# Attention output divided with features on partitions instead of after a transpose, and a half-precision product with wo

## The chip, the cores and the metric

The kernel runs on one core of a Trainium2 chip. Its engines are TensorE (PE in the profile, its weight loads PEld), VectorE (DVE), ScalarE (ACT), GpSimd (POOL) and SyncE (SP), which here issues DMAs. The metric is the device time of one execution in microseconds.

## The reference

Two blocks run one after the other on a sequence of 2048 tokens with 448 features: attention with 16 heads of 28 features, and a product-key mixture of experts that reads its result. Shapes: `x` 1 x 2048 x 448, `wqkv` 448 x 1344, `wo` 448 x 448.

```python
def _A_ref(x, wqkv, wo):
    B, S, D = x.shape
    H = 16
    Dh = D // H
    qkv = (x @ wqkv).reshape(B, S, 3, H, Dh).transpose(2, 0, 3, 1, 4)
    q, k, v = qkv[0], qkv[1], qkv[2]
    scores = jnp.einsum("bhqd,bhkd->bhqk", q, k) * (Dh ** -0.5)
    p = _softmax(scores, axis=-1)
    o = jnp.einsum("bhqk,bhkd->bhqd", p, v)
    return o.transpose(0, 2, 1, 3).reshape(B, S, D) @ wo
...
h = x + _A_ref(_layernorm(x), A_wqkv, A_wo)
h2 = h + _B_ref(_layernorm(h), B_w_q, B_k1, B_k2, B_u, B_v)   # 16 heads, two key tables of 64, top 8, 4096 experts
```

## The kernel before

**Stages.** First queries, keys and values are projected and written to memory (to about 155 us of the span). Then the attention runs (155 to 829 us), with much other work woven into it. After it come the rest of the mixture's preparation and the expert products.

**The attention.** The generator `attention` makes 256 steps: 16 blocks n, each with 16 key tiles k. Block n is a pair b, g: 512 queries (b, four of them) and four heads (g, four groups). Step u issues the scores of step u + 2 (L565, 12 matmuls on row tiles), the two exponentials for them (L569, on ScalarE) and the values of step u (L592, column tiles, accumulated in one PSUM bank called A over the 16 steps of a block). The four heads of a block lie on partitions 32j to 32j + 31: 28 features, then on row 32j + 28 the sum of the exponentials (values carry a column of ones), then three zeros. At some steps, the `paired` ones, the values of the following step run too. The scores have room for one and a half steps in PSUM.

**Dividing (`finish`, L572).** After a block's last step VectorE copies A to SBUF (`o`, L597). Two steps into the next block TensorE transposes `o` in four pieces into the PSUM bank M (L580), VectorE takes the reciprocals of the 16 sums a token now has (L582) and multiplies (L583) into `ob[b]`, tokens on partitions, 448 features. Bank M exists once during the attention and serves all side work: a new user waits until the one before it has been read. `behind_values` says at which steps `finish` is issued behind the values instead of ahead of them.

**The product with wo (`project(b)`, L640).** When the four blocks of b are divided, four tiles of 128 tokens follow, six steps apart. Each loads x, transposes its tile of `ob` (through `transposed` and `turn`, L122, into M), makes a high and a low fp32r part (L659, L136, L137), and multiplies: eleven matmuls of 448 columns with the high and low parts of wo (L93, as `M<-woh,oh`, `M<-wol,oh`, `M<-woh,ol`; the low part has three feature tiles). Then x is added (L680), the row moments taken (L730), a reciprocal root made on GpSimd (L113), and the normed row transposed by DMA (L699). `load_wo` (L627) reads wo in four slices through a tile with two buffers, and VectorE and GpSimd split it. For b = 3 the same runs after the attention, with `room`: more buffers, ScalarE for the copies.

**What is woven.** `weave` runs generators by positions: each has a number of steps and a stretch, and the one with the lowest position goes next. The order that comes out is the order on all engines and on SyncE's queue (manual schedule). Positions in the attention are its steps. Until step 68 (`FOLDED`) the fold of the query weights runs beside it; then from `begin[b]` the projection of b, and 26 steps later the search over the keys (`search`, 16 products of 11 matmuls, one every two steps, with weights loaded at L784 into three buffers, two of which serve one pair of products). `begin` is 73, 133 and 195. Splitting of the expert tables (`part`, on GpSimd), maxima over them (`tops`) and the choice of pairs (`pairs_of`) run beside all this.

**Scales.** `Scale.see` takes a maximum over the columns of a piece (L150), `spread` the maximum over pieces and copies it to a 128 x 128 tile, `share` has TensorE transpose that tile into M (L158) and then takes the overall maximum and makes a power of two from it. The fold's weights and the expert tables use it; wo doesn't.

**The tail.** After step 255: the copy, `finish` of block 15, then `project(3, 2, room)` woven with two first expert products (`first_up`), the first expert weights (`weights(0)`: VectorE compares L973, L979, L994, TensorE L1021) and the last search's scores (`kept_scores`).

## Time and profile before

| | us |
|---|---|
| three runs: median (lowest, highest) | 1591.58 (1589.65, 1596.7) |
| the profiled execution | 1590.46 |
| its span, first to last instruction | 1588.7 |

| engine | busy us in the span | share |
|---|---|---|
| PE | 1532.8 | 96% |
| PEld | 669.4 | 42% |
| DVE | 1146.5 | 72% |
| ACT | 910.0 | 57% |
| POOL | 362.1 | 23% |

The chain that ended last is 74% TensorE and 18% VectorE. These shares are means over stages with different limits, so they don't say what a change in one stage is worth; for that the stretches and the timelines are read. A matmul's row begins when it is issued and its end is modelled, so rows of consecutive matmuls overlap, and the time that one costs is read from the start of one to the start of the next.

### The profile page before, as it was taken

The numbers are of one execution on the slowest core, as the hardware profiler recorded it, in microseconds if no ns is written. First come the engines' busy times: TensorE is split into PE (matmuls) and PEld (weight loads), VectorE is DVE, ScalarE is ACT, GpSimd is POOL, SyncE is SP. The second block draws the span as 40 slices with busy tenths as digits, with TensorE's granted clock in tenths as the row PEclk, the third lists the DMA queues.
The fourth block names the chain that finished last, engine by engine and source line by source line (L and its number), as shares of the span: only waits on it lengthen the run. The fifth ranks groups of instructions, "written<-read, shape, count | busy, mean of one in ns | idle before, by whom it ended". The sixth has DMA issues, their size and how long they took to land.

```text
span 1588.7 us, 33185 instructions
## 1 busy us (share of the span) xinstructions
PE 1532.8 (96%) x12540; PEld 669.4 (42%) x12540; DVE 1146.5 (72%) x3924; ACT 910.0 (57%) x1220; POOL 362.1 (23%) x488
## 2 busy tenths in 40 slices
PE   5999999999999999999998999999999999999999
PEld 3444222233333333333335654455445554555444
DVE  7763365444477867666599899789998999789623
ACT  3544888888888888888873433344423344334322
POOL 1242000534235743787662000000000000000000
PEclk9999999999999999999999999999999999999999
DMA  8424687556677756569733244453344534443444
GB/s 278 141 97 127 224 268 244 173 179 215 213 252 218 245 173 219 165 202 278 225 114 101 91 133 130 130 182 119 105 136 129 158 107 132 141 137 117 121 144 134
DMA packets 170018, 266.10 MB, mean 167 GB/s; under 512 B 25472, under 2 KB 102016, under 8 KB 169856
## 3 DMA queue, kind: packets, MB, share of 16 engines
q1 hardware_dynamic: 165632, 261.88, 52.9%
q10 hardware_dynamic: 4224, 2.10, 0.4%
q8 instruction: 98, 1.61, 0.4%
q14 instruction: 64, 0.52, 0.1%
HBM read 211.88 MB, written 49.28 MB: 164 GB/s over the span
## 4 chain that ended last, share of the span: by engine, by line
PE 74%; DVE 18%; DMA 2%; POOL 2%; issue 2%; ACT 1%; SPq 0%; DVEq 0%; POOLq 0%
PE M L93 14%; PE acc L1234 14%; PE A L592 13%; PE S L565 11%; PE A L93 9%; PE pq L93 6%; DVE p L994 4%; DVE fg L979 2%; DVE G L1015 2%; PE M L273 2%; PE A L1021 1%; DVE ring L1206 1%; DVE f L973 1%; DVE w L1209 1%; PE A L1011 1%
## 5 line engine op out<-in xcount | busy, mean ns | idle before, releaser
L569 ACT ACTIVATE P<-S,escale 128x1024 f32<-128x1024 f32 x512 | 535.7, 1118 | 82.1 <-PE S L565 75.9
L1234 PE MATMUL acc<-v,w 128*128 128x448 f16 x1536 | 308.3, 354 | 1.3 <-DVE w L1209 1.0
L592 PE MATMUL A<-P,V 128*32 128x512 f32 x2048 | 257.6, 601 | 1.3 <-DVE o L597 1.3
L565 PE MATMUL S<-qS,kS 32*128 32x512 f16 x3072 | 230.4, 378 | 2.9 <-ACT P L569 2.2
L1234 PEld LDWEIGHTS <-w 128*128 128x128 f16 x1536 | 148.4, 98 | 143.4 <-DVE w L1209 4.0
L93 PEld LDWEIGHTS <-u 128*128 128x128 f16 x1386 | 131.1, 98 | 146.4 <-issue 6.8
L93 PE MATMUL A<-Xb,u 128*128 128x512 f16 x759 | 178.6, 384 | 2.5 <-DVE G L1015 2.5
L1160 ACT ACTIVATE ring<-A,ugelu 128x512 f32<-128x512 f32 x71 | 48.7, 687 | 218.8 <-PE A L93 218.8
L994 DVE TENSOR_TENSOR p<-st,iota 128x2048 f16<-128x2048 f16 x128 | 156.7, 1225 | 14.9 <-PE M L1011 8.1
L93 PE MATMUL M<-w,Xb 128*128 128x512 f16 x704 | 163.1, 379 | 3.5 <-DVE oh L137 1.6
L1206 DVE SCALAR_TENSOR_TENSOR ring<-ring,wscale,G 128x512 f32<-128x512 f32 x128 | 92.1, 746 | 77.7 <-ACT ring L1160 77.6
L565 PEld LDWEIGHTS <-kS 32*128 32x128 f16 x3072 | 63.6, 92 | 198.3 <-issue 162.7
L93 PE MATMUL M<-Xb,u 128*128 128x512 f16 x627 | 146.4, 379 | 0.0
L93 PEld LDWEIGHTS <-Xb 128*128 128x128 f16 x704 | 64.0, 98 | 92.8 <-issue 20.5
L1208 ACT ACTIVATE w<-ring 128x512 f16<-128x512 f32 x128 | 75.8, 622 | 41.1 <-DVE ring L1206 28.9
L592 PEld LDWEIGHTS A<-P,V 128*32 128x32 f32 x2048 | 48.2, 108 | 120.5 <-issue 110.9
L816 DVE MAX8 ti<-fresh 128x8 f32<-128x64 f32 x384 | 57.3, 212 | 53.8 <-ACT fresh L797 53.6
L1051 POOL TENSOR_SCALAR raw<-raw,scale 128x512 f32<-128x512 f32 (+1 forms) x64 | 47.4, 741 | 188.7 <-PE M L158 145.8
L1209 DVE SCALAR_TENSOR_TENSOR w<-w,ring 128x512 f16<-128x512 f16 x128 | 84.9, 686 | 7.2 <-ACT w L1208 6.9
L1160 ACT ACTIVATE ring<-M,ugelu 128x512 f32<-128x512 f32 x57 | 39.2, 688 | 87.8 <-PE M L93 86.1
L979 DVE TENSOR_TENSOR fg<-f,st 128x2048 f16<-128x2048 f16 x64 | 78.8, 1231 | 0.1
L818 DVE FIND_INDEX8 ti<-ti,fresh 128x8 uint32<-128x64 f32 x384 | 76.9, 220 | 0.0
(197 smaller groups left out, 1897.3 us busy)
## 6 DMA issues: line engine op xcount, KB each, us to landing
v<-vs SPq DMA_DIRECT2D x128, 336.0 KB, 2.9
u<-us SPq DMA_DIRECT2D x126, 256.0 KB, 2.6
w<-wp SPq DMA_DIRECT2D x56, 512.0 KB, 4.9
kS<-ks SPq DMA_DIRECT2D x64, 256.0 KB, 4.9
V<-vd SPq DMA_DIRECT2D x64, 256.0 KB, 3.6
wr<-in_wq_dram SPq DMA_DIRECT2D x32, 448.0 KB, 4.2
vs<-hl SPq DMA_DIRECT2D x32, 336.0 KB, 5.2
seen<-in_uT_dram SPq DMA_DIRECT2D x32, 256.0 KB, 5.0
```

Source lines behind the costliest of these rows:

```text
L93: nc.tensor.matmul(ps, l, r, start=i == 0, stop=i == len(pairs) - 1)
L565: nc.tensor.matmul(S[j // 2][:, j % 2], kS[r, a, 128 * (k % 4):128 * (k % 4) + 128], qS[r, c], start=m == 0, stop=m == 2)
L569: nc.scalar.activation(Pt[:, 2 * i:2 * i + 2], S[i], AF.Exp, scale=escale[:, n % 4:n % 4 + 1])
L592: nc.tensor.matmul(O[n][32 * j:32 * j + 32], V[:, k % 4, j], Pt[:, j], start=k == 0, stop=k == NT - 1)
L818: nc.vector.max_index(i, t, src)
L979: nc.vector.tensor_tensor(fg.rearrange("p t k f u -> p t k (f u)"), f1.rearrange("p t f u -> p t (f u)").unsqueeze(2).to_broadcast([128, T ...
L994: newest[0] = nc.vector.tensor_tensor(p1, pairs(0, s, TG, 128), ids(TG, 128), op=OP.is_equal).ins
L1160: gelu[0] = nc.scalar.activation(act, p, AF.Gelu_apprx_tanh, scale=ugelu).ins
L1206: nc.vector.scalar_tensor_tensor(av, av, wscale, of_expert(b, f), op0=OP.mult, op1=OP.mult)
L1208: nc.scalar.activation(w[:, 0], a, AF.Copy, scale=1.0 / LS)
L1209: newest[0] = nc.vector.scalar_tensor_tensor(w[:, 1], w[:, 0], -LS, a, op0=OP.mult, op1=OP.add).ins
L1234: nc.tensor.matmul(acc[j][:, :D], l, r, start=f == 0 and k == 0, stop=f == 31 and k == 2)
```

## The change

Division moves to where the features still lie on partitions, for 15 of the 16 blocks, and no transpose is made:

- The copy of A goes straight to `on[b]`, 128 x 4 x 512, for all four groups of b.
- `divide(n, k)` runs at the steps k of the following block. At k = 1 the four rows of sums are written to memory (`gather`, four rows of 2 KB).
- For n with n mod 4 = 3, at k = 2 each row of sums is loaded from memory onto its 32 partitions (`spread`, four DMAs), and at k = 4 to 7 VectorE takes the reciprocal of 128 columns and multiplies them (`scale`, four times).
- For the other blocks the 2048 sums are loaded as 128 x 16 at k = 3, inverted at k = 5, written back at k = 6, spread at k = 8, and multiplied at k = 10 over 512 columns.
- The last block has `divide_last`: four matmuls of 4 columns pick the sums out transposed, VectorE inverts and copies them 32 times wide, four transposes bring that back, and VectorE multiplies.
- A product tile takes its 128 columns of `on[b]` as they are: a half-precision copy, a subtraction for the low half, and twelve matmuls of half precision (four feature tiles for each of three products). wo is padded to 4 x 128 rows to match.
- Half precision needs a scale: `load_wo` now loads wo in one DMA, takes four maxima, shares them (with the transpose on TensorE), and splits on VectorE alone, in 9 calls over positions 0 to 8. The inverse scale is applied where x is added.
- `begin` becomes 76, 133 and 197; `behind_values` is gone.

```diff
-        def finish(n, o):
+        def gather(n):
             b, g = divmod(n, 4)
-            if g == 0:
-                ob[b] = (w2 if b % 2 else pp).tile([128, 4, D], F32, name="ob", bufs=1)
+            nc.sync.dma_start(sum_d[n], on[b].rearrange("(j r) g q -> j r g q", r=32)[:, 28, g])
+        def spread(n, src):
+            rb[n] = pp.tile([128, 512], F32, name="rb", bufs=1)
+            for j in range(4):
+                nc.sync.dma_start(rb[n][32 * j:32 * j + 32], src[j:j + 1].to_broadcast([32, 512]))
+        def invert(n, k):
+            flat = (lambda t: t.rearrange("j (k q) -> (j k) q", q=16))
+            if k == 0:
+                rb[n] = pp.tile([128, 16], F32, name="r", bufs=1)
+                nc.sync.dma_start(rb[n], flat(sum_d[n]))
+            elif k == 1:
+                nc.vector.reciprocal(rb[n], rb[n])
+            else:
+                nc.sync.dma_start(flat(rec_d[n]), rb[n])
+        def scale(n, c, inverse):
+            b, g = divmod(n, 4)
+            r, o = rb[n][:, c], on[b][:, g, c]
+            if inverse:
+                nc.vector.reciprocal(r, r)
+            nc.vector.scalar_tensor_tensor(o, o, onscale, r, op0=OP.mult, op1=OP.mult)
+        def divide(n, k):
+            if k == 1:
+                gather(n)
+            if n % 4 == 3:
+                if k == 2:
+                    spread(n, sum_d[n])
+                if 4 <= k < 8:
+                    scale(n, slice(128 * (k - 4), 128 * (k - 3)), True)
+            elif k in (3, 5, 6):
+                invert(n, (3, 5, 6).index(k))
+            elif k == 8:
+                spread(n, rec_d[n])
+            elif k == 10:
+                scale(n, slice(0, 512), False)
+        def divide_last(n):
+            b, g = divmod(n, 4)
+            o = on[b][:, g]
             flush()
-            pt = P[0].tile([128, 4, 4, 32], F32, name="M")
+            pt = P[0].tile([128, 4, 4], F32, name="M")
             for c in range(4):
-                nc.tensor.transpose(pt[:, c].rearrange("p h d -> p (h d)"), o[:, 128 * c:128 * c + 128], ident)
...
+                nc.tensor.matmul(pt[:, c], o[:, 128 * c:128 * c + 128], ct[:, C_SEL:C_SEL + 4], start=True, stop=True)
+            r = pp.tile([128, 4, 4], F32, name="r", bufs=1)
+            nc.vector.reciprocal(r, pt)
+            rr = pp.tile([128, 4, 4, 32], F32, name="rb", bufs=1)
+            nc.vector.tensor_copy(rr, r.unsqueeze(3).to_broadcast([128, 4, 4, 32]))
+            pt = P[0].tile([128, 4, 128], F32, name="M")
+            for c in range(4):
+                nc.tensor.transpose(pt[:, c], rr[:, c].rearrange("p j d -> p (j d)"), ident)
+            nc.vector.scalar_tensor_tensor(o, pt.rearrange("p c q -> p (c q)"), onscale, o, op0=OP.mult, op1=OP.mult)
...
     def load_wo():
...
+        S = Scale("o", 4)
+        raw = w2.tile([128, 4, 512], F32, name="on", bufs=1)...
+        nc.sync.dma_start(raw, wo)
+        yield
+        yield
+        for g in range(4):
+            S.see(g, raw[:, g])
+        yield
+        yield from S.share()
+        nc.vector.tensor_scalar(hscale, hscale, S.floor, 2.0 ** -TOP, op0=OP.mult, op1=OP.mult)
+        for g in range(4):
+            times(woh[:, g], raw[:, g], S.scale)
+            nc.vector.scalar_tensor_tensor(wol[:, g], raw[:, g], S.scale, woh[:, g], op0=OP.mult, op1=OP.subtract)
+            yield
+    WO = 9
...
-            of = transposed(ob[b][:, j])
-            oh = w2.tile([128, 4, 128], FR, name="oh2", bufs=1)
-            ol = w2.tile([128, 3, 128], FR, name="ol2", bufs=1)
+            of = on[b][:, :, c]
+            oh = w2.tile([128, 4, 128], F16, name="oh2")
+            ol = w2.tile([128, 4, 128], F16, name="ol2")
+            copy(nc.scalar if room else nc.vector, oh, of)
             if room:
-                nc.scalar.activation(oh, of, AF.Copy)
                 yield
-                halved()
-            else:
-                due.append(halved)
-                yield
+            nc.vector.tensor_tensor(ol, of, oh, op=OP.subtract)
+            yield
             yield
             flush()
             pa = P[0].tile([128, 512], F32, name="M")
-            mm_all(pa[:, :D], products(lambda t: oh[:, t], lambda t: ol[:, t], lambda t: woh[:, t], lambda t: wol[:, t]))
+            mm_all(pa[:, :D], [(l[:, t], w[:, t]) for l, w in ((oh, woh), (oh, wol), (ol, woh)) for t in range(4)])
...
-        begin = [FOLDED + 5, 67 + 66, 67 + 128]
+        begin = [FOLDED + 8, 67 + 66, 69 + 128]
```

## Rows read from the trace of the kernel before

**Rows 1.** Busy time by stretch: length, engines with counts, granted clock, DMA share, GB/s.

```profile
156.00:320.00 164.00, 161.26 (x1569) 45.62 (x1562) 81.57 (x170) 143.52 (x138) 20.20 (x29) 1.00 0.68 223
396.00:490.00 94.00, 93.66 (x816) 30.48 (x818) 57.22 (x433) 77.49 (x80) 37.33 (x48) 1.00 0.71 231
...
829.00:867.00 38.00, 30.03 (x294) 20.98 (x293) 32.47 (x49) 13.86 (x22) 15.89 (x21) 1.00 0.43 138
```

**Rows 2.** TensorE's timeline around one product tile: start, length, instruction, count.

```profile
362.39 1.08 PE L565 MATMUL S<-qS,kS 32*128 32x512 f16 x12
...
364.40 0.66 PE L122 MATMUL M<-ct,ob 128*128 128x128 f32 x4
364.99 0.83 PE L565 MATMUL S<-qS,kS 32*128 32x512 f16 x12
...
368.35 1.08 PE L93 MATMUL M<-woh,oh 128*128 128x448 f32 x4
...
370.79 0.83 PE L565 MATMUL S<-qS,kS 32*128 32x512 f16 x12
```

**Rows 3.** ScalarE's timeline in the first search, around one divided block.

```profile
435.98 2.12 ACT L569 ACTIVATE P<-S,escale 128x1024 f32<-128x1024 f32 x2
438.59 2.12 ACT L569 ACTIVATE P<-S,escale 128x1024 f32<-128x1024 f32 x2 [0.49 <-PE S L565]
...
441.83 2.12 ACT L569 ACTIVATE P<-S,escale 128x1024 f32<-128x1024 f32 x2
445.12 2.12 ACT L569 ACTIVATE P<-S,escale 128x1024 f32<-128x1024 f32 x2 [1.17 <-PE S L565]
```

**Rows 4.** TensorE's timeline in the first search: one product and what follows it.

```profile
438.43 2.55 PE L93 MATMUL M<-w,Xb 128*128 128x512 f16 x11
440.91 0.83 PE L565 MATMUL S<-qS,kS 32*128 32x512 f16 x12
```

**Rows 5.** TensorE's timeline behind the fold, steps 66 to 71.

```profile
318.78 0.66 PE L580 MATMUL M<-ct,o 128*128 128x128 f32 x4
319.37 1.07 PE L592 MATMUL A<-P,V 128*32 128x512 f32 x8
...
322.12 1.15 PE L565 MATMUL S<-qS,kS 32*128 32x512 f16 x12
...
324.20 1.08 PE L565 MATMUL S<-qS,kS 32*128 32x512 f16 x12
...
329.24 1.06 PE L592 MATMUL A<-P,V 128*32 128x512 f32 x8
```

**Rows 6.** Groups by line and shape, VectorE: busy us, mean ns, idle before.

```profile
L1206 DVE SCALAR_TENSOR_TENSOR ring<-ring,wscale,G 128x512 f32<-128x512 f32 x128 | 92.1, 746 | 77.7 <-ACT ring L1160 77.6
...
L150 DVE TENSOR_REDUCE tops<-seen 128x1 f32<-128x448 f32 x32 | 19.1, 602 | 0.1
...
L583 DVE TENSOR_TENSOR ob<-M,r 128x448 f32<-128x448 f32 x16 | 10.0, 624 | 0.6
...
L582 DVE RECIPROCAL r<-M 128x16 f32<-128x16 f32 x16 | 4.1, 257 | 22.6 <-PE M L580 22.5
...
L906 DVE RECIPROCAL sm<-sm 128x64 f32<-128x64 f32 x4 | 2.2, 552 | 0.1
```

**Rows 7.** TensorE's waits from 155 to 830 us: in total, times, longest.

```profile
PE M L580 <- DVE oh L137: 1.5, 1, 1.5
PE M L93 <- DVE oh L137: 1.4, 2, 1.2
```

**Rows 8.** SyncE's timeline: the first two slices of wo.

```profile
324.84 1.15 SPq L635 DMA_DIRECT2D wor<-in_wo_dram  x2
```

**Rows 9.** The line that loads wo (L635): landing times.

```profile
DMA to landing us min/median/max: 2.5/4.7/4.9
```

**Rows 10.** The line that loads the search's weights (L784): landing times.

```profile
DMA to landing us min/median/max: 3.6/4.9/8.3
```

More of the change, by code (lines that the diff above doesn't have):

```diff
@@ L31 @@
 TOP = 14
+OTOP = 5
 UP0 = 2
@@ L72, in block @@
     vs_d = [dram.tile([128, 3, D], F16, name=f"vs{f}") for f in range(32)]
+    sum_d = [dram.tile([4, 512], F32, name=f"sum{n}") for n in range(4 * NB)]
+    rec_d = [dram.tile([4, 512], F32, name=f"rec{n}") for n in range(4 * NB)]
     s_d = [dram.tile([128, 2, 1024], F16, name=f"sd{b}") for b in range(NB)]
@@ L85, in block @@
     escale = const.tile([128, 4], F32)
+    onscale = const.tile([128, 1], F32)
+    hscale = const.tile([128, 1], F32)
     lneps = const.tile([128, 4], F32)
@@ L363, in scale_wv @@
             times(vscale, S.floor, 2.0 ** -TOP / XS)
+            nc.vector.tensor_scalar(onscale, S.scale, ct[:, C_MASK:C_MASK + 1], 2.0 ** (OTOP - TOP), op0=OP.mult, op1=OP.mult)
+            times(hscale, S.floor, 2.0 ** -OTOP)
         def scale_wqk(g):
@@ L548, in block, with attention @@
     fold_p = fp.enter_context(tc.tile_pool(name="fold", bufs=2, reuse_waits="tile"))
-    ob = {}
-    def attention(paired, behind_values):
+    on = {}
+    def attention(paired):
         O = {}
@@ L679, in added @@
             def added():
-                nc.vector.tensor_tensor(xt, at if room else pa[:, :D], xt, op=OP.add)
+                if room:
+                    nc.vector.tensor_tensor(xt, at, xt, op=OP.add)
+                else:
+                    nc.vector.scalar_tensor_tensor(xt, pa[:, :D], hscale, xt, op0=OP.mult, op1=OP.add)
                 nc.sync.dma_start(h_d[4 * b + j], xt)
@@ L1107, in block @@
         w2 = r2.enter_context(tc.tile_pool(name="w2", bufs=2, reuse_waits="tile"))
-        woh = wo_p.tile([128, 4, D], FR)
-        wol = wo_p.tile([128, 4, D], FR)
-        work = [(a, 257 - FOLDED, 0, 257 - FOLDED), (load_wo(), 5, 0, 5)]
+        woh = wo_p.tile([128, 4, D], F16)
+        wol = wo_p.tile([128, 4, D], F16)
+        work = [(a, 257 - FOLDED, 0, 257 - FOLDED), (load_wo(), WO, 0, 8)]
         for b in range(3):
```

54 lines of the change are left out of this document (19 added, 35 removed).

## Prediction, made before the change was run

> **What bounds the kernel now.** I read the busy time by stretch first, then TensorE's and ScalarE's timelines inside the attention, then the waits of TensorE, then SyncE's DMA issues. The change touches only the attention stage (about 156 to 829 us of the span) and its tail up to about 870 us; afterwards the same instructions run in both kernels. In the stretches of [rows 1] TensorE is busy 98 to 100% and ScalarE 82 to 88%, at a granted clock of 1.00, so both could be the bound, and the timelines must decide step by step. A step of the attention without side work is one group of 12 score matmuls, 8 of values, and two exponentials. In [rows 5] score groups start at 322.12 and 324.20, 2.0 to 2.1 us apart: that is ScalarE's pace. A step that also carries a product or transposes is set by TensorE: in [rows 2] the score groups around the four transposes of L122 lie 2.60 us apart (362.39 to 364.99), and in [rows 3] ScalarE starts its pairs 2.61 and 3.24 us apart in the search and waits for scores. So TensorE work that goes away is worth its full length where TensorE sets the step (the search, the fold), and in a light step only the part above 2.05 us.
>
> **Transposes of the divided output (L580), 15 of 16 blocks.** Four transposes take 0.58 us from their first start to the next work ([rows 5]: 318.78 to 319.37). The last block keeps TensorE work of its own (tail, below). The blocks divided inside the fold (3) give the full 0.59. Those in the search (5): [rows 3] shows the pair at 441.83 followed after 3.29 us, where the same place without them (435.98) has 2.61, so 0.68 each; the extra 0.1 is the wait for the single PSUM bank M. The other seven stand in light steps, which fall from about 2.4 to the 2.05 floor: 0.4 each. Sum 1.8 + 3.4 + 2.8 = 8.0 us.
>
> **Transposes ahead of the product with wo (L122 on ob), 12 tiles inside the attention.** 2.60 less 2.05 gives 0.55 each ([rows 2]), 6.6 us.
>
> **The product.** Eleven matmuls on fp32r take 2.44 us from first start to the next scores ([rows 2]: 368.35 to 370.79). Twelve half-precision ones aren't in the trace at this place; the nearest row is the search's product ([rows 4]), 11 of 512 columns in 2.48 us, so 0.225 each, by 448/512 times 12 makes 2.37. I take 0.07 a tile, 0.8 us for 12 tiles; the bounds are 0 and 2.
>
> **Stalls that lose their cause.** TensorE waited 1.5 us for bank M behind L137 (a transpose of L580 that found M still unread) and 1.2 us for the parts of wo, which came in slices from a two-buffer tile ([rows 7]: the 1.5, and the longest of the 1.4). With no transpose in M, and wo loaded at once three steps earlier than its first use, I count 1.4 and 1.2.
>
> **A new wait: the scale of wo.** load_wo now looks at all of wo, spreads the maximum and has TensorE transpose it (Scale.share) before a scale exists. TensorE works in order: everything behind that transpose (scores, values, hence the exponentials) waits. By the woven positions (9 steps over 8 units, the fifth call at 4.0) it comes right behind the values of step 71, which are the last row of [rows 5], so at about 330.2. wo's load is the first issue of the new pool; before it left SyncE at 324.84 ([rows 8]), behind stores of the fold's split parts that wait for VectorE; those come 0.9 us earlier without block 3's division (L582 and L583, [rows 6]), and the detour's issues of block 3 take about 0.5 us of that back, so I take 324.4. Slices of 224 KB landed after 2.5 to 4.9 us ([rows 9]); 512 KB of the search took 3.6 to 8.3 ([rows 10]); for 0.9 MB I take 6.5 and keep 4.9 and 8.3. It lands at 330.9. VectorE then needs four maxima of 0.60 ([rows 6], L150), one chunk of block 3's division that is queued in between (1.2, below) and about 0.4 of spreading: 334.9. The transpose would have run at 329.8 (the fourth L580 is gone before it), so TensorE waits 5.1 us. ScalarE has about 0.9 us of exponentials left beyond its usual lead, and the transpose costs 0.3: net 4.5 us, bounds 2.5 and 6.5. Behind it the halves of wo cost VectorE about 4.6 us, ready well before the first product, seven light steps later.
>
> **VectorE.** A block before: copy, 0.26 of reciprocal, 0.62 of product ([rows 6], L582, L583). After, for twelve blocks: copy, the same reciprocal on 16 columns, 0.75 for 512 columns (L1206): 0.13 more, under TensorE's work. For blocks 3, 7 and 11 the reciprocal runs on 128 columns four times. L582 (16 columns, 257 ns) and L906 (64 columns, 552 ns) give 6.1 ns a column, so 0.95 us, with 0.25 for its product 1.2 us, 4.8 in all, four steps just ahead of that sequence's first tile. VectorE has room at block 3 and is nearly full at blocks 7 and 11; the tile's own halves get cheaper (no read of PSUM, one subtraction in place of two). If the cover fails, the first product of a sequence waits: 0 to 2 us twice. I charge 1.0.
>
> **The detour through memory.** Six or seven DMAs a block, each behind another: gather, reload as 16 columns, write back, four spreading ones. SyncE is in order, so each waits at its head for the one before or for VectorE, with key, value, weight and search loads queued behind; VectorE in turn holds its queue for the reload. They are placed two steps apart (4.0 to 5.9 us), about what landings take ([rows 9], [rows 10]). I charge 0.5 us in all, with 0 and 8 as ends.
>
> **Tail, 829 to 870.** VectorE is busy 32.5 of 38.0 us there and TensorE 30.0 ([rows 1], last row), so the chain of VectorE rules. The last block's division gains a broadcast copy (0.62 to 0.75) and four transposes (0.6) in series and loses the four of tile 0; the other three tiles lose theirs in TensorE's shadow. The first sequence starts three steps later and the third two; inside the attention that only swaps light and heavy steps, but the third's last search product now ends with the attention. I charge 1.0, ends minus 2 and plus 4.
>
> **Sum.** 8.0 + 6.6 + 0.8 + 1.4 + 1.2 = 18.0 gained; 4.5 + 1.0 + 0.5 + 1.0 = 7.0 lost; net 11.0. The profiled execution took 1590.46 us (span 1588.7 and 1.8 around it), 1.1 below the median of the three runs, inside their spread; 1590.46 less 11.0 is 1579.5.
>
> **Rivals.** (a) *wo in time*: if the load lands in 4.9 us and the maxima come sooner, the new wait shrinks to 1 or 2 us. For it: SyncE's queue at 324 was filled with splits that may leave earlier. Time 1576. (b) *Round trips*: the steps between DMA and user are too short, and VectorE's queue stands for each reload and each spread; 12 blocks with two such waits of 0.35 us make 8 us, time 1588. Against it: four to six microseconds against medians of 4.7 and 4.9. The 64-byte pieces appear in no row. The Trainium skill (DMA: Bandwidth & Descriptors, Specifications and Anatomy of one DMA) says that pieces below 512 B cost a read-modify-write, and that a DMA's fixed cost, some 2 us, is mostly the receipt of its write, worst into HBM; this detour does two such writes a block, which by that rule lengthens exactly this chain. (c) *Queue head, slower*: in the search a weight plane is reloaded when a product has left it and is needed about 6.5 us later, while its load takes 4.9 ([rows 10]), so 1.6 us are spare. If SyncE stands longer than that behind a division's wait when such a load comes, TensorE waits the rest; with all 24 loads of the three searches late by 0.9 us more than the spare, 21 us are lost: 1601. Against it: the waited events are mostly old when SyncE comes to them. (d) *No effect*: the light steps are wholly ScalarE's, so that only search and fold blocks pay (5.2 us) against 7.0 lost: 1592.
>
> **How the numbers follow.** Forecast 0.44 (own range 1575 to 1585), (a) 0.19, (b) 0.20, (c) 0.08, (d) 0.09. About 0.5% is what a measurement of this kernel can tell from no change, so the bound is 1583.6. Of the forecast four fifths lie below it, of (a) all, of (b) a tenth: faster 0.56. Slower by over 0.5% is (c) and little else, 0.08. The range leaves out the far side of (c) and (d) and the best of (a): 1571 to 1592.
>
> **What would show it.** Right: no score groups 2.6 us apart in the tiles; pairs of search steps at 5.85 us throughout; one TensorE wait of 3 to 6 us on the spread maximum near 327 us; no M wait behind L137. Wrong: that wait missing or over 7 us; TensorE or ScalarE waiting for search weights or keys more than 1.5 us in total; products waiting for their halves at the first tile; the tail longer than 42 us.

## The result, and the profile after

The changed kernel took 1599.46 us (median of eight runs, 1598.1 to 1602.8) beside 1593.06 us for the kernel before on the same chip: a ratio of 1.0037, 95% interval 1.0026 to 1.0048. The forecast was 1579.5 us, with a range of 1571 to 1592. The change makes the kernel slower by about 6 us instead of faster by 11. The profiled execution of after took 1600.6 us, span 1598.8, mean granted clock 0.99 (before 1590.46, 1588.7, 0.997).

Busy time by stretch of the kernel after, as in [rows 1] (length, engines with counts, granted clock, DMA share, GB/s):

```profile
156.00:320.00 164.00, 161.88 (x1573) 44.72 (x1566) 83.86 (x172) 144.71 (x139) 20.48 (x29) 1.00 0.73 230
396.00:490.00 94.00, 90.26 (x794) 27.55 (x786) 55.48 (x391) 76.33 (x77) 31.96 (x41) 1.00 0.76 239
829.00:874.00 45.00, 35.92 (x350) 19.71 (x348) 38.52 (x107) 17.33 (x28) 19.56 (x29) 0.96 0.33 106
```

In the search TensorE, busy 93.66 us of 94 before, now has 3.7 us without work. The tail is longer, with a clock of 0.96. What was taken away did go. This is TensorE's timeline around the product tile of [rows 2], after the change:

```profile
363.80 0.83 PE L574 MATMUL S<-qS,kS 32*128 32x512 f16 x12
364.56 0.93 PE L100 MATMUL M<-woh,oh 128*128 128x448 f16 x4
365.32 0.92 PE L100 MATMUL M<-wol,oh 128*128 128x448 f16 x4
366.08 0.92 PE L100 MATMUL M<-woh,ol 128*128 128x448 f16 x4
366.93 0.83 PE L574 MATMUL S<-qS,kS 32*128 32x512 f16 x12
```

No transposes stand ahead of it, and the product takes 2.37 us (364.56 to 366.93), as estimated. What came instead is in the table of TensorE's waits in the same stretch, 156 to 870 us (in total, times, longest), to be held against [rows 7]:

```profile
PE M L165 <- DVE every L161: 7.5, 2, 7.2
PE M L100 <- DMA w<-wp: 5.0, 2, 2.9
PE M L100 <- DVE oh L106: 3.3, 2, 2.2
PE A L652 <- DVE on L659: 2.4, 3, 0.8
PE M L636 <- DVE ti L873: 2.1, 1, 2.1
PE M L643 <- DVE rb L640: 1.3, 1, 1.3
```

To price each wait I laid the steps of both kernels side by side: a step is the time from one pair of exponentials to the next (as in [rows 3]), and its excess is what it takes beyond the same kind of step without a wait (2.0 us light, 2.6 and 3.2 in the search). By that table the end of the attention lies 3.05 us later (last exponentials at 828.84 instead of 825.79). Steps that stall add 24.1 us, so the rest gained 21.0; that figure is a remainder.

| Place in the kernel after | idle of TensorE, us | excess of the steps, us |
|---|---|---|
| transpose for wo's scale, steps 73 and 74 | 7.16 | 9.0 |
| search weights late, steps 108, 229, 230 | 2.11, 2.88 | 2.3 and 4.65 |
| halves of a tile late, steps 143 and 213 | 2.23, 1.03 | 4.0 and 1.1 |
| copy of bank A, steps 97, 113, 129 | 0.81 each | 3.1 |
| tail, 829 to 866 | 2.06, 1.31 | 3.7 |

Another 3.05 us came at 1442 us, in code that did not change, where the granted clock was 0.66 for five microseconds; of all the kept traces only this one shows a fall there. The 6.4 us between the medians agree with the 6.8 that stood before it.

**The wait for wo's scale.** Three views of the same place: TensorE's timeline, VectorE's, and busy time by stretch.

```profile
327.19 1.07 PE L652 MATMUL A<-P,V 128*32 128x512 f32 x8
335.41 0.48 PE L165 MATMUL M<-ct,every 128*128 128x128 f32 x1 [7.16 <-DVE every L161]
337.21 1.93 PE L652 MATMUL A<-P,V 128*32 128x512 f32 x8
```

```profile
331.25 2.20 DVE L157 TENSOR_REDUCE topso<-on 128x1 f32<-128x448 f32 x4 [7.72 <-DMA on<-in_wo_dram]
333.36 0.94 DVE L610 RECIPROCAL rb<-rb 128x128 f32<-128x128 f32 x1
334.34 0.37 DVE L611 SCALAR_TENSOR_TENSOR on<-on,onscale,rb 128x128 f32<-128x128 f32 x1
334.81 0.54 DVE L161 COPY every<-topo 128x128 f32<-128x128 f32 x1
```

```profile
328.00:332.00 4.00, 0.25 (x4) 0.00 (x0) 0.75 (x2) 1.40 (x2) 0.04 (x1) 1.00 0.81 276
332.00:336.00 4.00, 0.59 (x5) 0.32 (x9) 3.93 (x8) 0.00 (x0) 3.74 (x5) 0.57 0.03 11
336.00:340.00 4.00, 4.00 (x36) 0.63 (x30) 3.79 (x11) 2.12 (x2) 1.16 (x1) 0.58 0.00 0
```

The load left SyncE at 322.89 and VectorE could begin at 331.25, 8.4 us later. The four maxima, one chunk of block 3's division in VectorE's queue and the spreading follow as drawn in the prediction. The values at 337.21, eight matmuls, take 1.93 us instead of 1.07: behind the idle the granted clock averages 0.58 from 336 to 340 us, for most of that stretch the lower of its two levels (1.2 GHz of 2.4). The size of the idle varies: the four other runs that left this place alone have 5.49, 6.30, 6.60 and 7.03 us.

**Late search weights.** SyncE's timeline ahead of the two late loads (L841), and TensorE's waits for them:

```profile
415.09 2.06 SPq L592 DMA_DIRECT2D rb<-rec  x4
417.25 0.84 SPq L841 DMA_DIRECT2D w<-wp  x2
...
741.95 0.32 SPq L772 DMA_DIRECT2D xd<-Xb  x1
...
744.74 0.89 SPq L586 DMA_DIRECT2D sum<-on  x1
745.72 0.90 SPq L841 DMA_DIRECT2D w<-wp  x2
```

```profile
422.81 1.02 PE L100 MATMUL M<-w,Xb 128*128 128x512 f16 x4 [2.11 <-DMA w<-wp]
...
751.44 1.02 PE L100 MATMUL M<-w,Xb 128*128 128x512 f16 x4 [2.88 <-DMA w<-wp]
752.40 1.47 PE L574 MATMUL S<-qS,kS 32*128 32x512 f16 x12
```

In the first case four spreading DMAs hold SyncE for 2.06 us just ahead of the weights, and the two stores of projected tiles (L772, L773) leave a little before them, at 412.09 and 412.66. In the second SyncE issues nothing from 737.93 to 741.95, standing for the transposes that the same stores must follow; the gather of the detour comes on top.

**Halves of a tile.** TensorE at the second tile of sequence 1:

```profile
523.50 1.51 PE L100 MATMUL M<-woh,oh 128*128 128x448 f16 x4 [2.23 <-DVE oh L106]
524.80 1.70 PE L100 MATMUL M<-wol,oh 128*128 128x448 f16 x4
```

Four matmuls take 1.5 to 1.7 us instead of 0.93: here, too, the clock fell behind the wait.

**The copy of bank A.** TensorE at the first of the three places:

```profile
391.70 1.07 PE L652 MATMUL A<-P,V 128*32 128x512 f32 x8 [0.81 <-DVE on L659]
```

The first values of a block stand here right behind the last of the block before, until VectorE has copied the bank.

### The profile page after: what moved, and what is told of

Read it like the earlier page. It is cut to its first block, busy times and chain, and to the rows that moved or that the text cites. A ratio compares the mean times of both kernels' runs of the same rounds, so it can differ in the third digit from the quotient of the medians.

```text
span 1598.8 us, 33145 instructions
## 1 busy us (share of the span) xinstructions
PE 1528.5 (96%) x12441; PEld 646.8 (40%) x12441; DVE 1169.8 (73%) x3944; ACT 908.4 (57%) x1220; POOL 361.2 (23%) x484
## 4 chain that ended last, share of the span: by engine, by line
PE 70%; DVE 21%; DMA 3%; POOL 2%; issue 2%; ACT 1%; SPq 1%; DVEq 0%; POOLq 0%
PE acc L1290 14%; PE A L652 12%; PE M L100 12%; PE S L574 11%; PE A L100 9%; PE pq L100 6%; DVE p L1051 4%; DVE G L1072 2%; DVE fg L1036 2%; PE M L280 2%; DVE f L1030 1%; DVE ring L1262 1%; DVE pos L875 1%; PE A L1078 1%; DVE w L1265 1%
## 5 line engine op out<-in xcount | busy, mean ns | idle before, releaser
L574 PE MATMUL S<-qS,kS 32*128 32x512 f16 x3072 | 237.2, 380 | 3.0 <-ACT P L578 2.2
```

The source lines that it names most:

```text
L574: nc.tensor.matmul(S[j // 2][:, j % 2], kS[r, a, 128 * (k % 4):128 * (k % 4) + 128], qS[r, c], start=m == 0, stop=m == 2)
```

## The experiments

Each edit is made on the changed kernel unless said otherwise. Ratios are to the kernel before.

**wo's maximum taken in the fold**

```
+    WOS = Scale("o", 4)
+    def tops_wo():
+        for k in range(7):
+            if k < 4:
+                raw[k] = sp.tile([128, 512], F32, name="seen", bufs=4)
+                nc.sync.dma_start(raw[k][:, :D], wo[:, k])
+            if k >= 3:
+                WOS.see(k - 3, raw.pop(k - 3)[:, :D])
+            yield
...
+              (tops_wo(), 7, 46, 55), (WOS.share(), 3, 56, 59),
...
-        for g in range(4):
-            S.see(g, raw[:, g])
-        yield
-        yield from S.share()
+        yield
+        yield
+        yield
```

> The changed kernel with the maximum of wo, its spreading and its transpose taken in the fold, from four slices, some 12 steps earlier; the load of all of wo and its halves stay where they were. Theory (the wait for wo's scale and the fall of the clock behind it cost 9 us): TensorE no longer idles before the transpose of the spread maximum (7.16 us in the changed kernel), steps 73 and 74 take about 2.0 us each instead of 10.19 and 2.75, the granted clock stays at 1.00 between 332 and 340 us, and the time falls from 1599.5 by 8 to 9.5 us to about 1591. Rival 1 (my sum's size, 4.5 us net, the rest of that stretch being lost anyway): 1595. Rival 2 (VectorE's backlog only moves to the first product with wo, whose parts then come late): TensorE waits 2 to 5 us at the first product of sequence 0 instead, 1596 to 1598.

1593.69 us, ratio 1.0007 (0.9995 to 1.0019): 0.30% below the change, 4.8 us. TensorE's timeline at the place, and the stretch:

```profile
330.26 1.06 PE L652 MATMUL A<-P,V 128*32 128x512 f32 x8
331.26 1.08 PE L574 MATMUL S<-qS,kS 32*128 32x512 f16 x12
```

```profile
332.00:336.00 4.00, 4.00 (x46) 0.96 (x40) 3.29 (x5) 4.00 (x5) 2.49 (x3) 1.00 0.70 226
```

Steps 73 and 74 take 1.99 and 2.00 us and the clock stays up: at its place the wait cost 8.95 us, as the theory has it, idle and clock together. The whole gained less: the transpose now waits for bank M in the fold (step 59, 1.25 more), step 108 took 0.9 more, and 1.8 us came in the first steps of the attention, where no instruction differs. There the granted clock was at its lower level around 160 us, as it was near that place in eleven of the eighteen kept traces, one of them of the kernel before with an edit that works far behind. Rival 2 falls: no wait at the first product of sequence 0.

**The first projection one step later (odd)**

```
-        begin = [FOLDED + 8, 67 + 66, 69 + 128]
+        begin = [FOLDED + 9, 67 + 66, 69 + 128]
```

> The changed kernel with the first projection one step later (step 77 instead of 76), nothing else. Its paired steps (the values of two units in one step) then fall on even steps, so the last values of a block and the first of the next no longer run back to back; and the reloads of the first search's weights fall one step later, away from the four spreading DMAs. Theory (parity and queue): TensorE's three waits for the copy of bank A (0.81 us each, about 1.0 us of the step each) vanish, and so does the wait for a search weight at step 108 (2.11 us): 5 us less than 1599.5, about 1594.5. Rival 1 (parity only): 3 us less, 1596.5. Rival 2 (the later search overlaps the second projection by one step more, and VectorE's backlog at step 143 grows by what the others give): 1599 to 1601.

1598.73 us, ratio 1.0032 (1.0016 to 1.0048). Both mechanisms of the theory are there: the three waits for bank A are gone (1.02 to 1.04 us of step each), and so is that for the weight at step 108 (2.3). TensorE at the place where the first copy was waited for, and at the second tile of sequence 1:

```profile
392.64 1.92 PE L652 MATMUL A<-P,V 128*32 128x512 f32 x16
...
520.78 1.67 PE L100 MATMUL M<-woh,oh 128*128 128x448 f16 x4 [4.11 <-DVE oh L106]
```

The 5.1 us gained by step 134 were mostly given back: step 143 takes 9.75 us instead of 7.12 and step 155 4.52 instead of 3.23. That is rival 2, with the theory's gain ahead of it.

**The detour at other steps**

```
-            if k == 1:
+            if k == (1 if n % 4 == 3 else 3):
                 gather(n)
...
-            elif k in (3, 5, 6):
-                invert(n, (3, 5, 6).index(k))
-            elif k == 8:
+            elif k in (5, 7, 8):
+                invert(n, (5, 7, 8).index(k))
+            elif k == 11:
                 spread(n, rec_d[n])
-            elif k == 10:
+            elif k == 13:
```

> The changed kernel with the detour of the twelve blocks at other steps: gather 1 to 3, reload 3 to 5, reciprocal 5 to 7, write 6 to 8, the four spreading DMAs 8 to 11, the product 10 to 13, so that none of the larger groups of issues stands just ahead of a reload of a search weight. Theory (SyncE's queue, held for up to 2 us by the detour's issues, makes two search weights late): TensorE's two waits for w (2.11 us at step 108, 2.89 us at step 229, the second with a fall of the clock) vanish, 6 to 7 us less than 1599.5, about 1593. Rival 1 (only the first is the detour's, the second is the stores of the projected tiles and a load of 5.7 us): 2 to 3 us less, 1597. Rival 2 (the weights would be late anyway, by contention of the transfers): within 1 us of 1599.5.

1609.62 us, ratio 1.0104 (1.0087 to 1.0121): none of the three, 10 us worse. VectorE's timeline and then TensorE's tell why:

```profile
392.24 0.75 DVE L611 SCALAR_TENSOR_TENSOR on<-on,onscale,rb 128x512 f32<-128x512 f32 x1 [6.06 <-DMA rb<-rec]
...
396.65 0.68 DVE L659 COPY on<-A 128x512 f32<-128x512 f32 x1
```

```profile
397.39 1.07 PE L652 MATMUL A<-P,V 128*32 128x512 f32 x8 [2.95 <-DVE on L659]
```

VectorE stood 6.06 us at the head of its queue for the spread, and behind it lay a tile's halves and the copy of bank A, for which TensorE waited 2.95. That is the prediction's rival (b), made to happen: it needs other work of VectorE queued behind the standing. TensorE's waits for search weights fell from 5.0 us to 3.0 in all, so part of the theory came true, at a higher price.

**Blocks 3, 7 and 11 divided through TensorE**

```
+            if n in (3, 7, 11):
+                if k in (2, 4):
+                    divide_last(n, k // 2)
+                return
```

The first half of divide_last is the small matmuls, the reciprocal and the broadcast copy, the second the transposes and the product. The next experiment has all 15 blocks in the list.

> The changed kernel with blocks 3, 7 and 11, the fourth of each sequence, divided as the last block is: four small matmuls, a reciprocal of 16 columns and a broadcast copy in step 2, four transposes of the reciprocals and the product in step 4. This takes away their gather and spreading DMAs and twelve reciprocals of 128 columns (0.95 us each on VectorE). Theory (VectorE's backlog from these reciprocals makes the first halves of sequences 1 and 2 late): TensorE's waits for oh (2.23 us at step 143, 1.03 at step 205) vanish, the clock stays up at 523 us, 4 to 5 us gained, and the transposes put back cost 0.7 each, 2 us, so 2 to 3 us less than 1599.5, about 1597. Rival (the backlog comes from search 0, which now overlaps the second projection by three steps, and from the choice of pairs): the waits stay over half, and the time is 1599.5 to 1601.5. The wait for wo's scale should shrink by about one chunk (1.3 us), as a chunk of block 3's division stands in VectorE's queue ahead of it.

1602.01 us, ratio 1.0049 (1.0030 to 1.0067). Step 143 falls from 7.12 to 3.13 us, so the division of block 7 on VectorE is what makes the halves late there. The wide reciprocals are the larger part of what this edit takes from VectorE; it also takes the spread of their sums away, for which VectorE stood 1.5 us in all, in three places. But the route costs more than I gave it: the steps with the matmuls and the transposes take 1.4 and 1.5 us more each in the search and 1.3 together in light steps. The wait for wo's scale shrinks by 1.8.

**No detour at all**

> The changed kernel without any detour through memory: all 15 blocks of the attention divided as the last is, by four small matmuls, reciprocal, broadcast copy (step 2), four transposes of the reciprocals and the product (step 4). Everything else, the half-precision product and the scale of wo among it, is as in the changed kernel. By my sum the transposes put back cost 8.0 us and the small matmuls 1 to 3 more. Theory (the detour's cost is local: two late search weights, 6 to 7 us, and the halves at the first tiles, 4 to 5 us): these are won back, so the time is within 2 us of 1599.5. Rival 1 (the detour was nearly free, 1.5 us): 1608 to 1610. Rival 2 (the detour lengthens many steps by transfers in each other's way): 1592 to 1595.

1626.61 us, ratio 1.0207 (1.0190 to 1.0224), above all three. The two late weights and the late halves of step 143 are gone but for 0.5 us at step 108 (steps 108, 229 and 143 lose 1.6, 3.7 and 4.0), as the theory says; but the route through TensorE costs 1.2 to 2.9 us a block, and steps 183, 213 and 247 take 2.1 to 4.3 us more than in the changed kernel. TensorE's timeline at block 6:

```profile
455.56 1.05 PE L641 MATMUL M<-ct,on 128*128 128x4 f32 x8
456.96 2.53 PE L100 MATMUL M<-w,Xb 128*128 128x512 f16 x11 [0.35 <-DVE r L643]
...
462.80 0.66 PE L651 MATMUL M<-ct,rb 128*128 128x128 f32 x4
464.30 2.53 PE L100 MATMUL M<-w,Xb 128*128 128x512 f16 x11 [0.84 <-DVE on L652]
```

Four small matmuls run as eight, in 1.05 us, and each time the product behind them must wait until VectorE has emptied bank M. So this run doesn't price the detour; it says that this way around it is dearer by far.

**Three odd beginnings**, on the kernel with wo's maximum in the fold

```
+        begin = [75, 135, 197]
```

> The kernel with wo's maximum taken in the fold (1593.7 in its runs), and the projections beginning at steps 75, 135 and 197 instead of 76, 133 and 197: all odd, and each search over before the next projection. Theory: beside the wait for wo's scale, the three waits for bank A's copy (3 us), the late search weight at step 108 (2.3 to 3.3) and the wait for the halves of the first tile of sequence 1 (2.23 us and the fall of the clock, 4) vanish: 1593.7 less 9 is 1584.5. Rival 1 (the halves wait for the 128-column reciprocals of block 7, wherever the search lies; the parity is right): 1588.5. Rival 2 (what one wait gives back another takes, because the transfers and VectorE are full): 1592 to 1595.

1592.45 us, ratio 0.9994 (0.9985 to 1.0003). The waits for bank A are gone; the halves at the first tile of sequence 1 are not (3.15 us; step 139 takes 7.99), although the first search is over. So they are not late because of the overlap, and weights were late at steps 107 and 123 beside 229.

**The same with the detour at 3, 5, 7, 8, 11 and 15, and with its last product alone moved from 10 to 12**

> The previous kernel with the detour of the twelve blocks at other steps: gather 3, reload 5, reciprocal 7, write 8, spread 11, product 15, that is two steps for the first landing, three for the write and four for the spread. In the earlier test of other steps VectorE stood 6.06 us for the spread, two steps after its issue, and held the copy of bank A back by 2.95 us; here four steps lie between. Theory (queue and standing): the late search weight at step 229 (4.6 us with the clock) vanishes, because the gather no longer stands ahead of it, and VectorE's waits for the spread fall from 17 us to under 5: 4 to 5 us below the previous kernel, 1580. Rival 1 (the weight at step 229 is late by the stores of the projected tiles, not by the gather): within 1.5 us of the previous kernel. Rival 2 (other loads, of keys and values, now stand behind the detour): 2 to 6 us above it.

> The kernel with wo's maximum in the fold and beginnings 75, 135 and 197, and of the detour the last product alone moved, from step 10 to 12, so that the spread has four steps to land instead of two; SyncE's order is as in that kernel. It tells VectorE's standing for the spread from SyncE's order. Theory (VectorE's 17 us of standing lie in steps where it has room, and cost next to nothing): within 1.5 us of the kernel with the product at step 10. Rival (the standing feeds VectorE's backlog, and so the waits for copies and halves): 2 to 4 us less than that kernel.

The first took 1594.16 us, ratio 1.0007 (0.9993 to 1.0021): step 229 still 8.24 us with the gather out of the way (rival 1), and TensorE's waits for search weights 10.3 us, six times, instead of 5.0 (rival 2). The second took 1590.22, ratio 0.9975 (0.9964 to 0.9986), 0.19% below the kernel with the product at step 10; SyncE's order is the same in both. By the medians VectorE's standing thus costs 2 to 3 us, but the intervals just touch, and the two profiled executions don't show it: the last exponentials start at 823.66 us here and at 817.89 there. Of these 5.8 us some 1.7 lie in the opening, and the rest mostly in steps 139, 167 and 229, where halves and weights come later than in the other. What the standing costs by itself stays open.

**The stores of the projected tiles four steps later**

```
-        if not room:
-            store_X(b)
...
+            work += [(look, SEARCH, t, t + SEARCH), (stored(b), 1, t + 4, t + 5)]
```

> The changed kernel with the two stores of a sequence's projected tiles four steps later, nothing else. In the changed kernel SyncE stands 4.0 us at step 224 for the transposes that those stores must follow, and the search weight issued behind them makes TensorE wait 2.89 us at step 229, with a fall of the clock. Theory (it is that standing, since with the gather moved away step 229 still took 8.24 us): step 229 takes about 3.2 us instead of 6.92, step 230 2.6 instead of 3.58, 4 to 4.7 us gained, 1595 in place of 1599.5. Rival (the landing of 5.7 us alone makes it late): 1598 to 1599. The wait at step 108 (behind the four spreading DMAs, and later behind the stores) stays or grows.

> The kernel before the change, with the stores of the projected tiles four steps later and nothing else. It tells whether that remedy mends something that the change brought, or something that the kernel had all along. Theory (the change brought it: before, SyncE stood for the keys' bank ahead of these stores and no longer at them, and the search weights there came 0.15 us late): within 1.5 us of 1593.4. Rival (the stores held the queue before too): 2 to 4 us less, by steps 227 (3.55) and 239 (4.72).

On the changed kernel 1597.17 us, ratio 1.0016 (1.0002 to 1.0029). SyncE's timeline, then TensorE's, at the load that was late second; it left at 745.72 in the changed kernel:

```profile
738.30 1.83 SPq L843 DMA_DIRECT2D w<-wp  x2
```

```profile
743.08 2.55 PE L100 MATMUL M<-w,Xb 128*128 128x512 f16 x11
```

The product runs through. Steps 229 and 230 lose 4.65 us, as expected, and step 108 its 2.3 as well, which I had not expected: there too the stores stood in SyncE's queue ahead of the weights. The four spreading DMAs still do. By the steps 6.9 us, by the medians 0.2% or 3.4; opening steps that differ by up to 1.8 us and late falls of the clock of 3, both in code that is the same, blur a difference of this size. On the kernel before the same edit gives 0.9992 (0.9983 to 1.0001), no difference: the remedy mends what the change brought. Which part of the change brought it at step 229 is not shown. With the gather moved away TensorE still waited 3.50 us there; of the runs that leave the stores in place only the one without any detour, whose steps are longer, had that weight in time; and all of them begin the third projection at step 197 instead of 195, which was not tried apart.

**The second projection at step 137**

```
+        begin = [76, 137, 197]
```

> The changed kernel with the second projection at step 137 instead of 133, nothing else: four light steps more between the reciprocals of block 7 and the first halves, and the first search over before it. Theory (VectorE's backlog from reciprocals, search, pairs and maxima drains in those steps): the wait for the halves (2.23 us and the fall of the clock at step 143, 3.9 us in all) falls under 0.5 us: 1595.5 in place of 1599.5. With the beginning at 135 and an earlier first search the wait was still 3 to 4 us, so two steps are not enough. Rival (the halves wait for the load of all VectorE's work there, which moves along): a wait of over 2 us near step 143 or 147, 1598.5 to 1600.5.

1603.44 us, ratio 1.0055 (1.0040 to 1.0071). The wait at step 143 vanished and came back as stalls at steps 146, 159 and 213 (4.03, 5.37 and 6.85 us; the first for the copy of bank A, the others for halves): the rival. VectorE's backlog moves along with the search that now ends beside the next reciprocals.

**All remedies together, then the tail, then 135 again**

> All single remedies in one: wo's maximum in the fold, beginnings 75, 137 and 197, the last product of the detour two steps later, the stores of the projected tiles four steps later. The kernel with the first three and 135 in place of 137 took 1590.2. Theory (each remedy works on its own wait): TensorE's waits between 330 and 825 us for wo's scale, bank A, the halves and the search weights fall under 4 us in all, 1590.2 less 6 for the halves and 5 for weights at steps 107 and 229, so 1579 to 1582, which is what my sum expected of the change. Rival (transfers and VectorE are full, and the waits come back elsewhere): 1586 to 1591.

> The previous kernel with the last two of the third search's maxima called later: one behind the copy of the last block, one behind its division. In the changed kernel the four small matmuls of the last block wait 2.06 us because VectorE copies the block only after five such maxima in a row. Theory: the copy comes at about 1.2 us after the last values instead of 2.5, the first matmul of the experts 1 to 1.7 us earlier, and the granted clock may stay up at 838 us: 1 to 3 us less than the previous kernel. Rival (VectorE does the same work in another order, and the halves of the last sequence's tiles come as late as before): within 0.7 us.

> All remedies in one as in the kernel at 1587.4 (wo's maximum in the fold, the last product of the detour at step 12, the stores of the projected tiles four steps later), but the second projection at step 135 instead of 137, so that the second search ends two steps before the third projection instead of with its beginning. In the kernel with 137 TensorE still waited 8.8 us for halves, at steps 141, 153, 213 and 219. Theory (VectorE's backlog around the wide reciprocals of blocks 7 and 11, made longer by whatever search ends beside them): the waits at steps 213 and 219 (5.42 and 4.79 us steps) fall to the level of the kernel with 135 before (no step there over 3.7 us), the one at step 139 is as there (8 to 9 us): 1585 to 1588. Rival (the waits follow the transfers and not the end of the search): steps 213 and 219 stay over 4.5 us.

1587.41 us, ratio 0.9949 (0.9929 to 0.9968): inside the rival's range. Waits for wo's scale, bank A and weights are gone (0.2 us left), but the halves wait 8.8 us in four places, so VectorE remains. With two of the last search's maxima moved behind the last block's copy and division, 1587.21 (0.9950, 0.9934 to 0.9966): the wait at L636 falls from 2.0 to 0.9 and nothing is gained, as the rival says: a wait for a normed row behind it (L129) grows from 1.19 to 3.09. With 135 in place of 137: 1585.10 (0.9948, 0.9932 to 0.9964), by the ratio the same as with 137; step 213 falls to 4.06 (3.7 expected) and step 219 to the ordinary, and step 139 takes 9.79. TensorE there:

```profile
502.83 1.68 PE L100 MATMUL M<-woh,oh 128*128 128x448 f16 x4 [3.90 <-DVE oh L106]
```

**VectorE relieved there**

```
-(tops(VS, lambda f: v[:, f], D), TOPS, 44, 88)
+(tops(VS, lambda f: v[:, f], D), TOPS, 4, 48)
```

> The kernel before this in the list (all remedies, beginning 135) with the loads and the 32 maxima of the second expert matrix taken over steps 72 to 116 instead of 112 to 156; each maximum is 0.6 us of VectorE, 19 us in all, and they lie between the reciprocals of block 7 and the first halves of sequence 1. Theory (the halves are late because VectorE is full there, not because of the detour's transfers): the wait at step 139 (3 to 4 us, 8 to 9 us for the step) falls under 1 us, 5 to 6 us gained: 1580 to 1583. Rival 1 (the halves wait for the spread of the sums itself, which lands 4 to 5 us after its issue): no change at step 139. Rival 2 (the maxima now crowd the first projection and search): as much lost between steps 75 and 115 as won at 139.

1582.90 us, ratio 0.9924 (0.9911 to 0.9937). VectorE's timeline, then TensorE's:

```profile
493.99 0.95 DVE L610 RECIPROCAL rb<-rb 128x128 f32<-128x128 f32 x1 [3.24 <-DMA rb<-sum]
...
504.46 0.94 DVE L610 RECIPROCAL rb<-rb 128x128 f32<-128x128 f32 x1
505.43 0.35 DVE L611 SCALAR_TENSOR_TENSOR on<-on,onscale,rb 128x128 f32<-128x128 f32 x1
505.70 0.42 DVE L106 CAST oh<-on 128x512 f16<-128x512 f32 x1
```

```profile
506.18 0.93 PE L100 MATMUL M<-woh,oh 128*128 128x448 f16 x4 [1.51 <-DVE oh L106]
```

The wait falls from 3.90 to 1.51 and step 139 from 9.79 to 4.72, with the detour untouched: most of the lateness is VectorE's work. The edit moves the matrix's loads along with the maxima, but the spread came no sooner for it: block 7's first reciprocal starts 10.8 us ahead of step 139 in both executions, and the fourth 2.1 us into that step with the maxima and 0.3 us ahead of it without. Search weights came late at steps 111 and 123, beside the moved loads (5.6 us, rival 2). The two profiled executions therefore end the attention alike (814.2 us); the medians differ by 2.2 us, the intervals touch.

**The four chunks one step later**

```
-                if 4 <= k < 8:
+                if 5 <= k < 9:
```

> The kernel at 1582.9 (all remedies, the second expert matrix's maxima earlier) with the four chunks of the division of blocks 3, 7 and 11 one step later each (steps 5 to 8 of the next block instead of 4 to 7). There VectorE stood 3.24 us for the spread of block 7's sums before the first chunk, and the first product of sequence 1 still waited 1.51 us, step 139 taking 4.72 us. Theory (the rest of that wait is this standing, and the fourth chunk then comes behind the first halves): step 139 takes about 3.2 us, 1.5 us gained, 1581 to 1582. Rival (the chunks now crowd the first tile's halves instead): step 139 unchanged within 0.5 us or longer.

1582.87 us, ratio 0.9931 (0.9913 to 0.9948). TensorE at the first tile of sequence 1:

```profile
503.31 0.93 PE L100 MATMUL M<-woh,oh 128*128 128x448 f16 x4 [0.16 <-DVE oh L106]
```

Step 139 takes 3.36 us: the rest of the wait was VectorE's standing for the spread of block 7's sums and the fourth chunk ahead of the halves. The time is the same as without this edit within the intervals. With all of it the kernel is 0.7% faster than before, 11 to 12 us. The gains of the change are real, and its new waits ate most of them and more. That the result is the size of the forecast is a coincidence: waits remain, the gains were larger than counted, and the earlier maxima, worth 2 to 4 us here, were not tried on the kernel before.

## Why the prediction was wrong, by its own steps

The gains held and the price of the new waits failed: 7.0 us were charged for it and 27.8 measured (wo's scale 9.0, search weights 6.9, halves 5.1, bank A 3.1, tail 3.7).

**What bounds the kernel** held. Light steps take 1.99 us, ScalarE's pace, and work taken from TensorE counted as it was split up.

**The gains** were right. The first four blocks gave 2.1 us where 2.2 were counted; in the search 0.68 a block, as counted; 0.45 to 0.5 for each tile's transposes instead of 0.55, 0.07 for the product. All gains up to the end of the attention are 21.0 us, against 18.0. The surplus lies in stalls that I had not counted: steps 210 and 239 of the kernel before (3.98 and 4.72 us) have no counterpart after.

**The wait for wo's scale**, 4.5 us with bounds of 2.5 and 6.5, measured 9.0. Two terms of that step failed. The landing was mis-sized: 8.4 us instead of 6.5, just beyond the end kept from [rows 10], and that is the idle of 7.16 instead of 5.1. (Load and transpose both came some 1.5 us earlier than reckoned, because the blocks divided in the fold had already gained 2 us; this cancels.) By the prediction's own working 7.16 us of idle nets 6.6, about its upper end. And the clock was left out, which is most of the remaining 2.4: the steps behind the idle ran at the lower level. Taking the wait away gave 8.95 us back.

**"Inside the attention that only swaps light and heavy steps"** is wrong. Beginning at step 76 instead of 73 makes the paired steps odd, and at three block ends the values of two blocks then run back to back on the one bank A. Nothing in the sum stood for that; 3.1 us, shown by moving the beginning by one.

**The detour**, 0.5 us with 8 as the end: two late search weights cost 6.9. Rival (c) has the right mechanism and the wrong number of places: two of 24 loads, where SyncE was held by the four spreading DMAs or by stores. I looked at the 1.6 us to spare of a load, not at what precedes each load in SyncE's queue. Both weights came in time with the stores four steps later, so the 6.9 is not the detour's alone: the larger part, 4.65 at step 229, is SyncE's standing for the stores, for which the sum had no term, with the gather on top. That 6.9 lies inside the 0 to 8 is therefore partly luck. On rival (b) the Trainium skill was cited (DMA: Bandwidth & Descriptors, Anatomy of one DMA: a fixed cost of some 2 us, mostly the receipt of the write, heaviest into HBM; that section is about DMAs issued by GpSimd, and here SyncE issues them). The detour's writes of reciprocals landed after 2.4 to 4.6 us and the spreads after 1.9 to 4.1, which allows that; no run here separates the receipt from the wait in line. VectorE stood 17.3 us for spreads and 7.7 for reloads in the kernel after, three times what rival (b) counted; what that cost by itself is open, as said above.

**VectorE**, 1.0 us with 0 to 2 twice, measured 5.1. The chunk's product takes 0.35 us and not 0.25, but the step that failed is "VectorE has room": I put the reciprocals beside an average, while the maxima of the second expert matrix, the search's and the choice of pairs lie in the same steps. Taking block 7's division off VectorE, or the matrix's maxima, removed most of the wait at the first tiles. And the wait brings a fall of the clock, 1.7 us at step 143.

**The tail**, 1.0 with an end of 4, measured 3.7, inside its bounds: the four small matmuls behind five maxima in VectorE's queue, as the prediction feared of the third search, and a clock of 0.72 from 836 to 842 us. Moving two maxima did not bring it back, so VectorE's total work may be what sets the tail; that is argued from one run and not shown.

**The range.** All upper ends together (2.0 for wo, 7.5 for the detour, 3 for VectorE, 3 for the tail) reach 1595, and it stopped at 1592. Of the 4.5 us beyond, 2.6 are the base: the sum starts from one execution at 1590.46, and beside the changed kernel the median of the kernel before is 1593.06. The rest is the bank and the clock behind the waits, less the 3 us by which the gains were larger. The fall of the clock at 1442 us, which the medians don't need, and those near 160 us in the opening stay open: they come and go between executions, and no run here sets them off. Whether the earlier maxima would also help the kernel before was not tried.

## What to carry to other kernels

When a change takes work off the engine that sets the pace and puts waits into the queues of others, the gains are the easy half: list for every new instruction that waits what is queued behind it on its engine, and for every moved loop which steps now fall together. Price a wait of the matrix engine with and without a slow stretch behind it; here 7.16 us of idle cost 9.0 and 2.88 cost 4.65, but 2.99 at step 108 of the kernel with wo's maximum in the fold, where the clock stayed up, cost 3.15. A value that only needs the data early, such as a scale, is best taken where slices of the data can pass by long before its use.

## What the runs showed of the hardware

TensorE's granted clock fell to the lower of its two levels (1.2 of 2.4 GHz; 0.57 to 0.61 in the stretches around 334, 526 and 754 us) behind idles of 7.16, 2.23 and 2.88 us, but not behind the 2.11 us at step 108, where the scores that follow take 0.83 us as ever. The Trainium skill (TensorE: Matmul & The Clock Gate, The HAM clock gate) says that the slow level is the default and that activity lifts it; these rows agree with that. The length of an idle alone does not tell whether the clock falls. TensorE at step 108 of the kernel with wo's maximum in the fold, then at step 143 of the kernel with the stores four steps later:

```profile
417.94 1.02 PE L100 MATMUL M<-w,Xb 128*128 128x512 f16 x4 [2.99 <-DMA w<-wp]
```

```profile
519.78 1.16 PE L100 MATMUL M<-woh,oh 128*128 128x448 f16 x4 [1.88 <-DVE oh L106]
520.73 1.70 PE L100 MATMUL M<-wol,oh 128*128 128x448 f16 x4
```

Behind 2.99 us the granted clock stayed at 1.00 (418 to 422 us), behind 1.88 it was 0.57 (520 to 524).

Twelve half-precision matmuls of 448 columns take 2.37 us where eleven on fp32r took 2.44 [rows 2]. A small matmul of 4 columns in fp32 costs 0.26 us (four, run as eight, in 1.05), more than a transpose of 128 columns (four in 0.66). A load of 0.9 MB beside others could be used 8.4 us after its issue; those of 0.5 MB landed after 3.5 to 8.0.
